# Turning the keys of seven units by VectorE and a trip through DRAM instead of by TensorE

## The chip, the core and the metric

The kernel runs on one core of one Trainium2 chip, in one launch. The metric is the device time of that core in microseconds (us). All data are float32 in the kernel's tiles.

## What is computed

The reference is a gated linear attention, followed by a two-layer MLP with a quick GELU:

```python
# q, k, v, f_logit: (B=4, H=8, S=768, D=48);  moe_w_in (384, 2048);  moe_w_out (2048, 384)
f = 1 / (1 + exp(-f_logit))
for t in range(S):
    state = f[:, :, t, :, None] * state + einsum('bhd,bhe->bhde', k[:, :, t], v[:, :, t])
    y[:, :, t] = einsum('bhd,bhde->bhe', q[:, :, t], state)
x = y.transpose(0, 2, 1, 3).reshape(3072, 384)
h = x @ w_in
out = (h * (1 / (1 + exp(-1.702 * h)))) @ w_out
```

## The kernel before, in words

**Units.** The 3072 tokens are cut into 12 units (NALL) of 256 tokens (U), three for each batch. A unit n goes through `attention(n)`, which gives a list of parts, and later through `mlp_unit(n)`, which gives a list of small matmul jobs, the fill. For n from 4 on, `merge(n, ...)` emits the parts of unit n's attention one by one and, after each part, a share of the fill: the columns of one MLP unit (23040) split in proportion to a number for each kind of part. The fill that runs beside attention n is the end of an older unit's MLP and the beginning of the next. Its jobs come in two sorts. An `h` job (L727) is three matmuls of 256 columns over the three chunks of `w_in`, a sigmoid by ScalarE into `sg` (L732) and a product by VectorE into `g` (L733). An `o` job (L704) is one matmul of 192 columns; seven groups of eight of them, with sums between, make the second layer. In the trace each such float32 matmul leaves two records, so an `h` job shows as 6 and an `o` job as 2.

**Attention of a unit.** Queries, keys and gates of the unit lie in `X` and `F` with feature rows on the partitions and the 4 x 256 columns of 4 pairs of heads (NP) along the free dimension. From unit 3 on (N_FILL), three parts of kind V each do two of the six levels of the scan: scores by TensorE (L384), `promote` by VectorE, which multiplies queries and keys by gates (L439), `evacuate` by VectorE, which masks the scores into `A` (L410), and, one part later, `adds` by TensorE (L448). After the last `promote` the keys in `X[:, 1]` are complete.

**Turning the keys.** The step that brings a unit's keys and values together into states (part S, L523, `pd`) contracts over tokens, so it wants the keys with tokens on the partitions, as the tile `kn`. Two parts of kind T call `turn_k`: four TensorE transpositions of 128x128 into one PSUM tile of the pool tag "mm" (4 buffers, shared with `h` and `o`), then one ScalarE copy of 128x512 into `kn` (L505, L506). `kn` has one buffer, which a later `yT` uses too.

**Starting the next unit.** The parts of kind B of unit n belong to unit n+1. `begin_f` transposes the gates from `raw` into `F` by VectorE (L327, a STREAM_TRANSPOSE of 128x1024 in blocks of 32x32), applies the sigmoid by ScalarE and orders the next unit's gates (4 DMAs on SP's queue); `begin` does so for the queries, with two small GpSimd copies; `begin_k` does it for the keys, into `X[:, 1]`, which is free only when the previous unit's keys have been turned. `begin_k` also copies level 0 aside and makes the first `promote`. `begin_gates`, by GpSimd, multiplies gates together into `tot` (L376).

**The order of a unit n from 4 to 10 before:** V, V, V, B (begin_f, begin of n+1), T, T, B (begin_k of n+1), S (with begin_gates of n+1). The last unit, 11, has V, V, V, T, T, S, W. The shares after each part are those of `steady`.

**Who sets the order.** TensorE executes exactly the order in which the code emits (L89). From L903 on the other engines, SP's DMA queue included, are ordered by a planner, which works with its own costs: an instruction that is ready in its plan can be taken before others that the code emitted earlier but that are not ready. All DMAs that the kernel starts go through one queue, SP's, in the planned order, and an instruction of SP that waits holds those behind it.

**The rest of SP's queue in the stretch around the change:** `vl` (L290) and `vn` (L304), the values of the next unit; `raw` (L258), the next gates, queries and keys; `xT<-yT` (L592, L597), the attention's result on its way to the MLP; `out_dram<-osb` (L765), the result.

Of the kernel before, what the change touches and what calls it, by code (L numbers as in the profile page):

```python
# [9 lines left out]
F32 = mybir.dt.float32  # L10
# [13 lines left out]
def kernel(  # L24
# [33 lines left out]
    nc = tc.nc  # L58
    B, H, S, D = q.shape
    DM = H * D  # L60
    DFF = moe_w_in.shape[1]
    P = 128
    C = 64
    G = 128
    U = 256
    NG = U // G
    NC = U // C
    NU = S // U
    NP = H // 2
# [3 lines left out]
    NK = DM // P  # L73
    NFF = DFF // P
    FG = 4
    PAIRS_AHEAD = 3
    N_FILL = 3
    N_TURN = 2
    NA = NP * U
    NALL = B * NU  # L80
    assert S % U == 0 and NALL % 2 == 0 and NL == 6 and NG == 2 and DM % P == 0 and D <= HS

    const = ctx.enter_context(tc.tile_pool(name="const", bufs=1))
    ld = ctx.enter_context(tc.tile_pool(name="ld", bufs=1))
    att = ctx.enter_context(tc.tile_pool(name="att", bufs=1))
    wp = ctx.enter_context(tc.tile_pool(name="wp", bufs=2))
    mlp = ctx.enter_context(tc.tile_pool(name="mlp", bufs=2))
# [44 lines left out]
    X = const.tile([P, 3, NX], F32, name="X")  # L132
# [6 lines left out]

    w_in = const.tile([P, NK, DFF], F32, name="w_in")  # L140
    w_out = const.tile([P, NFF, DM], F32, name="w_out")
    v_toks = [tc.dram_tile([U, DM], F32, name=f"v_tok{j}") for j in range(2)]
    D2, DR = 2 * D, P - 2 * D
    assert NP == NK + 1 and NK * DR == D2
# [5 lines left out]
    for r in range(NGR):  # L150
        ffs = range(r * FG, (r + 1) * FG)
        for ff in ffs[::2]:
            f = slice(ff * P, (ff + 2) * P)
# [90 lines left out]
    def load_raw(n, j, engine=nc.sync):  # L244
        if n >= NALL:
            return
        b, s0 = n // NU, n % NU * U
        src = (f_logit, q, k)[j]
        if n < N_FILL:
            for a in range(NP):  # L250
                engine.dma_start(
                    out=by_pair[j][32 * a:32 * (a + 1), :, :R * D],
                    in_=src[b, 2 * a:2 * a + 2, s0:s0 + U, :].rearrange("h (i j) d -> i h (j d)", j=R),
                )
            return
        for r in range(4):
            lo = 32 * (r % 2)
            engine.dma_start(  # L258
                out=raw[32 * r:32 * (r + 1), j, :, :R * D - lo],
                in_=src[b, r // 2::2, s0:s0 + U, :].rearrange("a (i j) d -> i a (j d)", j=R)[:, :, lo:],  # L260
            )
# [3 lines left out]
    def order_v(n, engine=nc.sync):  # L265


        if n >= NALL or n < N_TURN:
            return
# [6 lines left out]
    def load_vl(n, l):  # L276

        if n >= NALL:
            return
# [12 lines left out]
    def load_vn(n):  # L292
        if n >= NALL:
            return
# [11 lines left out]
    def rows(h):  # L306
        return slice(h * HS, h * HS + D)
# [5 lines left out]
    def attention(n):  # L313
# [5 lines left out]
        t = {"tms": [F]}  # L319
        parts = []  # L320

        def part(kind):
            return lambda fn: parts.append((kind, fn))
# [174 lines left out]
        def turn_k(a0):  # L498
            if a0 == 0:
                t["kn"] = att.tile([P, NP, NG, P], F32, tag="kn", name=f"kn_{n}", bufs=1)  # L500
            pt = ps.tile([P, 2, NG, P], F32, tag="mm", name=f"tkn_{n}_{a0}", bufs=4)
            for a in range(2):
                for g in range(NG):
                    x = (a0 + a) * U + g * G
                    nc.tensor.transpose(pt[:, a, g, :], X[:, 1, x:x + G], ident)  # L505
            nc.scalar.copy(t["kn"][:, a0:a0 + 2], pt)  # L506

        for a0 in (0, 2):
            part("T")(lambda a0=a0: turn_k(a0))

        @part("S")
        def _():
# [34 lines left out]
        def _():  # L547
# [24 lines left out]
            to_x(lambda h: (yT[rows(h), :NK], lambda r, d: yT[r:r + d, NK]), xT[:, :, :U], NG)  # L572
            if n == NALL - 1:

# [31 lines left out]
    HF, HC = NFF // 2, DM // 2  # L606
    T = {}

    def quarter(w, i, j, ffs=slice(0, HF)):
        return w[:, i * HF + ffs.start:i * HF + ffs.stop, j * HC:(j + 1) * HC]  # L610

    def sums_of_b():


        for i in (1, 2, 3):
            T[i] = wp.tile([P, 2 * DM * 2], I32, tag="bits", name=f"T{i}", bufs=PAIRS_AHEAD)
            T[i] = T[i].bitcast(F32).rearrange("p (f e) -> p f e", f=HF)
        n4 = DM // HC
        t4 = [wp.tile([P, DM], F32, tag="a", name=f"T4_{f}", bufs=4).rearrange("p (f e) -> p f e", f=n4)
              for f in range(0, HF, n4)]  # L620
        T[4] = lambda f: t4[f // n4][:, f % n4]
        sub = lambda *x: nc.vector.tensor_tensor(*x, ALU.subtract)
        h = [slice(f, f + HF // 2) for f in (0, HF // 2)]
        for x in h:
            yield lambda x=x: sub(T[1][:, x], quarter(w_out, 0, 1, x), quarter(w_out, 0, 0, x))
        for x in h:
            yield lambda x=x: sub(T[2][:, x], quarter(w_out, 1, 1, x), T[1][:, x])
        for x in h:
            yield lambda x=x: sub(T[3][:, x], quarter(w_out, 1, 1, x), quarter(w_out, 0, 1, x))
        for i in range(len(t4)):  # L630
            x = slice(i * n4, (i + 1) * n4)
            yield lambda i=i, x=x: sub(t4[i], T[2][:, x], quarter(w_out, 1, 0, x))
# [165 lines left out]
    def mlp_blocks(*blocks):  # L798

        hs, os = zip(*(mlp_block(n, r) for n, r in blocks))  # L800
        return sum(hs, []) + sum(os, [])
# [12 lines left out]
    def parts_of(n):  # L814

        parts = list(units[n][1])
        _, inter = parts.pop()
        if n:
            kind, scores = parts[0]
            _, ahead = units[n - 1][1][-1]  # L820
            parts[0] = kind, lambda: (ahead(), scores())
        if n < N_TURN:

            def with_v(l):
                kind, fn = parts[l]
                return kind, lambda: (fn(), load_vl(n, l) if n == 0 or l else None, keep_up(2 * (n == 0 and l < 3) or 3 * (n == 1 and l == 0)))
            parts[:NL] = [with_v(l) for l in range(NL)]
        if n + 1 < NALL:
            begin_f, begin, begin_k, begin_gates = units[n + 1][0]
            i = len(parts)  # L830
            if n + 1 < N_FILL:

                parts.append(("K", lambda: (begin_k(), begin_gates(), load_vl(n + 1, 0) if n + 1 < N_TURN else None)))
                parts.insert(i - 4, ("B", begin))
                parts.insert(i - 5, ("B", begin_f))
            else:
                kind, states = parts.pop()
                parts += [("B", begin_k), (kind, lambda: (states(), begin_gates()))]
                parts.insert(i - 3, ("B", lambda: (begin_f(), begin())))
        else:  # L840
            parts.append(("W", inter))
        return parts

    def merge(n, fill, columns, share, pieces=0, hold=0, by=1.0, chores=()):

        parts = parts_of(n)
        total = sum(share(kind) for kind, _ in parts)
        converting = {"W": 3, "T": 3, "B": 1} if n < N_FILL - 1 else {"W": 3, "V": 4, "S": 3, "T": 1, "B": 1}  # L850
        total_ops = sum(converting.get(kind, 0) for kind, _ in parts)
        held = sum(share(kind) for kind, _ in parts[:hold])
        at = at_ops = done = ops = 0
        for kind, fn in parts:
            ready = state["done"]
            fn()
            for chore in chores[:2]:
                chore()
            chores = chores[2:]
            at += share(kind)  # L860
            at_ops += converting.get(kind, 0)
            n_ops = min(int(pieces * NOP * at_ops / (by * total_ops)), pieces * NOP) - ops
            ops += n_ops
            first, n_columns = done, max(0, columns * (at - held) / (total - held) - done)

            def some(end):
                nonlocal done
                while fill and done < end and fill[0][2] <= ready:
                    w, emit, _ = fill.pop(0)
                    emit()  # L870
                    done += w
            for i in range(n_ops):
                some(first + n_columns * i / n_ops)
                convert()
            some(first + n_columns)

    def steady(kind):
        return {"W": 3, "V": 4, "S": 3, "T": 1, "B": 1, "K": 1}.get(kind, 0)

    UNIT = NFF * NK * U + U // P * NFF * DM  # L880

    for j in range(3):
# [12 lines left out]
    fill = []  # L895
    merge(0, fill, 0, steady, 8)
    fill += mlp_blocks((0, 0)) + mlp_blocks((0, 1))
    merge(1, fill, UNIT // 2 - LAG // 2, steady, 10, hold=1)
    fill += mlp_blocks((1, 0), (1, 1)) + mlp_blocks((0, 2), (1, 2))
    merge(2, fill, UNIT, steady, 8)  # L900
    fill += mlp_blocks((2, 0), (2, 1)) + mlp_blocks((2, 2), (0, 3)) + mlp_blocks((1, 3), (2, 3))
    merge(3, fill, 3 * UNIT // 2 - LAG // 2, steady, 6, by=0.7)
    fill_order.close()  # L903
    for n in range(3, NALL):
        fill += mlp_unit(n)
    for n in range(4, NALL):
        merge(n, fill, NFF * NK * U + 7 * HF * HC, steady, chores=list(sums_of_b()) if n == 4 else ())
    for _, emit, _ in fill:
        emit()

# [28 lines left out]
```

## Time and profile before

| what | value |
|---|---|
| median of 4 runs | 658.45 us (656.46 to 661.61) |
| the profiled execution | 661.61 us, of which its span is 659.5 us |
| granted TensorE clock | 0.992 |
| TensorE transpositions for `kn` (L505) | x96, mean 273 ns, union of their records 14.1 us |
| ScalarE copies into `kn` (L506) | x24, mean 584 ns |
| VectorE transpositions 128x1024 (L327) | x18 into X, mean 2042 ns; x9 into F, mean 2051 ns |
| ScalarE copies 128x512 from X (L423) | Kc x69, mean 669 ns; Qc x27, mean 641 ns |

The span is the time from the first to the last record on the core. Busy time is the union of an engine's records. A matmul's record is longer than the distance to the next one's start, because matmuls are pipelined; where the cost of some matmuls on a full TensorE is wanted, starts are compared with starts. In the timeline, columns are start, length, engine, line, operation, output and inputs, shapes and count of merged records; in brackets stands the idle time before, with what ended it. The examples are taken from the attention of one late unit, between 335 and 384 us.

### The profile page before, as it was taken

Reading aid. Unit: us, or ns where it says so; the run is one execution under the profiler, and the core shown is the slowest. Engines: PE = TensorE matmul, PEld = TensorE weight load, DVE = VectorE, ACT = ScalarE, POOL = GpSimd, SP = SyncE. Lnnn points to the kernel's source line nnn. Section 1 sums busy time; section 2 is a strip of 40 time slices with the busy share of each in tenths; the row PEclk is TensorE's granted clock in tenths of the full one; section 3 lists DMA queues with packets and bytes.
Section 4 is the critical chain, followed back from the end, with each engine's and each line's share of the span. In section 5 each row is a group of like instructions: output and inputs, shape, how many; then the busy total and the mean of one; then the engine's idle time right before and its main releaser. Section 6 shows DMA issues by size and latency. Waiting matters only on the chain.

```text
span 659.5 us, 20407 instructions
## 1 busy us (share of the span) xinstructions
PE 639.1 (97%) x8964; PEld 545.0 (83%) x8964; DVE 444.8 (67%) x802; ACT 230.1 (35%) x477; POOL 54.0 (8%) x116
## 2 busy tenths in 40 slices
PE   6988999989999999999999999999999999999997
PEld 5655667766677689989989989989989989989997
DVE  2998887688886757657657657658558557553571
ACT  3563543243223423423423424324324324222120
POOL 3020020010001002002002002002002002000000
PEclk9999999999999999999999999999999999999999
DMA  8795973384116453524524434514613202101000
GB/s 184 197 230 155 230 181 96 110 199 98 41 41 176 121 121 95 143 73 99 151 59 116 122 74 119 148 43 119 158 34 95 74 25 59 42 2 25 25 1 24
DMA packets 67554, 67.67 MB, mean 103 GB/s; under 512 B 30410, under 2 KB 61290, under 8 KB 67466
## 3 DMA queue, kind: packets, MB, share of 16 engines
q1 hardware_dynamic: 67466, 66.38, 40.3%
q8 instruction: 70, 1.15, 0.7%
q14 instruction: 18, 0.15, 0.1%
HBM read 56.92 MB, written 8.65 MB: 99 GB/s over the span
## 4 chain that ended last, share of the span: by engine, by line
PE 85%; DVE 7%; DMA 2%; ACT 2%; SPq 2%; issue 1%; DVEq 0%; ACTq 0%
PE h L727 37%; PE o L755 7%; PE o_X L704 7%; PE o_Y L704 7%; PE o_Z L704 7%; PE sc L384 5%; PE y L448 5%; PE o_W L704 4%; PE y L563 2%; PE sc L523 1%; PE tkn L505 1%; DMA xT<-yT 1%; DMA vn<-in_v_dram 1%; DVE X L439 1%; PE t L339 1%
## 5 line engine op out<-in xcount | busy, mean ns | idle before, releaser
L727 PE MATMUL h<-xT,w_in 128*128 128x256 f32 (+1 forms) x1152 | 261.7, 383 | 6.0 <-DMA xT<-yT 3.7
L727 PEld LDWEIGHTS h<-xT,w_in 128*128 128x128 f32 x1152 | 216.4, 191 | 40.3 <-issue 5.0
L733 DVE TENSOR_TENSOR g<-h,sg 128x256 f32<-128x256 f32 (+1 forms) x192 | 80.9, 423 | 101.5 <-ACT sg L732 99.1
L732 ACT ACTIVATE sg<-h 128x256 f32<-128x256 f32 (+1 forms) x192 | 73.2, 383 | 195.8 <-PE h L727 189.0
L423 ACT COPY Kc<-X 128x512 f32<-128x512 f32 x69 | 46.1, 669 | 119.4 <-DVE X L439 83.4
L755 PE MATMUL o<-w_out,g 128*128 128x384 f32 x192 | 66.4, 493 | 0.0
L439 DVE TENSOR_TENSOR X<-X,tot 128x1024 f32<-128x1024 f32 x45 | 55.1, 1225 | 15.4 <-PE sc L384 10.2
L755 PEld LDWEIGHTS o<-w_out,g 128*128 128x128 f32 x192 | 35.2, 190 | 22.8 <-issue 1.5
L704 PE MATMUL o_X<-w_out,g 128*128 128x192 f32 x288 | 51.9, 329 | 0.0
L704 PE MATMUL o_Y<-T,S 128*128 128x192 f32 x288 | 51.1, 331 | 0.1
L704 PEld LDWEIGHTS o_Y<-T,S 128*128 128x128 f32 x288 | 46.5, 190 | 2.5 <-DVE u L679 1.2
L704 PEld LDWEIGHTS o_X<-w_out,g 128*128 128x128 f32 x288 | 47.3, 190 | 0.9
L410 DVE TENSOR_TENSOR A<-sc,masks 128x512 f32<-128x512 f32 x72 | 46.8, 680 | 0.0
L448 PE MATMUL y<-A,vl 64*48 64x64 f32 x2304 | 40.8, 217 | 0.1
L376 POOL TENSOR_TENSOR tot<-F 128x512 f32<-128x512 f32 x12 | 12.5, 1040 | 327.3 <-DVE st L540 327.3
L448 PEld LDWEIGHTS y<-A,vl 64*48 64x48 f32 x2304 | 36.0, 120 | 3.5 <-issue 3.1
L327 DVE STREAM_TRANSPOSE X<-raw 128x1024 f32<-128x1024 f32 x18 | 36.8, 2042 | 2.5 <-PE y L563 2.5
L571 ACT COPY yT<-y 48x512 f32<-48x512 f32 x48 | 27.8, 580 | 13.0 <-PE y L563 12.5
L384 PEld LDWEIGHTS sc<-X,Kc 48*64 48x64 f32 x1344 | 23.9, 134 | 7.1 <-issue 3.4
L384 PE MATMUL sc<-X,Kc 48*64 48x64 f32 x1344 | 28.2, 220 | 0.2 <-DVE A L410 0.2
L376 POOL TENSOR_TENSOR tot<-tot 128x256 f32<-128x256 f32 (+4 forms) x60 | 27.0, 450 | 4.7
L704 PE MATMUL o_Z<-w_out,g 128*128 128x192 f32 x144 | 26.6, 331 | 0.0
(93 smaller groups left out, 664.2 us busy)
## 6 DMA issues: line engine op xcount, KB each, us to landing
vl<-v_tok SPq DMA_DIRECT2D x60, 192.0 KB, 2.8
bits<-in_moe_w_out_dram SPq DMA_DIRECT2D x8, 768.0 KB, 11.1
bits<-in_moe_w_in_dram SPq DMA_DIRECT2D x8, 576.0 KB, 7.0
v_tok<-in_v_dram SPq DMA_DIRECT2D x10, 384.0 KB, 4.3
vn<-v_tok SPq DMA_DIRECT2D x10, 384.0 KB, 6.9
xT<-yT SPq DMA_DIRECT2D x24, 144.0 KB, 2.8
raw<-in_f_logit_dram SPq DMA_DIRECT2D x18, 192.0 KB, 4.2
raw<-in_q_dram SPq DMA_DIRECT2D x18, 192.0 KB, 3.9
```

The costliest lines, as they stand in the source:

```text
L327: nc.vector.transpose(out.rearrange("p (a i j) -> p a j i", a=NP, j=R), raw[:, j].rearrange("p a (j d) -> p (a j) d", j=R)[:, :, :32],)
L376: nc.gpsimd.tensor_tensor(tn, t2[:, :, 0], t2[:, :, 1], ALU.mult)
L384: nc.tensor.matmul(out[g * HS:(g + 1) * HS, h, a, :], lhsT=lhs(h, a * U + g * G), rhs=rhs(h, a * U + g * G), start=True, stop=True,)
L410: nc.vector.tensor_tensor(A[:, :, c:c + w].rearrange("p h (x t) -> p h x t", t=64), t["sc"][:, :, c:c + w].rearrange("p h (x t) -> p h x t ...
L423: nc.scalar.copy(c.rearrange("p (n m) -> p n m", m=m), X[:, j, :NA].rearrange("p (n two m) -> p n two m", two=2, m=m)[:, :, hf, :],)
L439: nc.vector.tensor_tensor(qk, qk, by, ALU.mult)
L448: nc.tensor.matmul(dst(h, g, a), lhsT=vls[n, u][g * 64:(g + 1) * 64, (2 * a + h) * D:(2 * a + h + 1) * D], rhs=A(h, g, a), start=(start an ...
L704: nc.tensor.matmul(t[bank], lhsT=lhs(f), rhs=rhs(f), start=(new and f == 0), stop=(f == HF - 1), skip_group_check=True,)
L727: nc.tensor.matmul(ph, lhsT=w_in[:, c, ff * P:(ff + 1) * P], rhs=xTs[n][:, c, :], start=(c == 0), stop=(c == NK - 1))
L732: nc.scalar.activation(sg, ph, AF.Sigmoid, scale=1.702)
L733: nc.vector.tensor_tensor(g[ff // FG][:, ff % FG, :], ph, sg, ALU.mult)
L755: nc.tensor.matmul(t["po"], lhsT=g[ff // FG][:, ff % FG, tt * P:(tt + 1) * P], rhs=w_out[:, ff, :], start=(ff == ffs[0]), stop=(ff == ffs[ ...
```

## The change

For units 4 to 10 (`CARRY`) the keys are turned in another way. Two VectorE transpositions in 32x32 blocks (one for each group of 128 tokens) write a tile `z`; four DMAs for each carry `z`, 32 partitions at a time, to a DRAM buffer `k_tok` in runs of 512 bytes; one DMA for each group reads it back with tokens on all 128 partitions in runs of 2 KB; one ScalarE copy of 128x512 for each group rearranges it into `kn`. The parts T, T become C (first transposition and its four DMAs) and C2 (second one with its four, and the reading back with the copies). The part B with `begin_f` and `begin` moves behind C2. From unit 4 on, all units use shares of their own, `late`. Units 0 to 3 and 11 keep TensorE's transpositions.

```diff
+    CARRY = range(N_FILL + 1, NALL - 1)
...
+    k_toks = [tc.dram_tile([NG, G, P // 32, 32 * NP], F32, name=f"k_tok{j}") for j in range(2)]
...
-        for a0 in (0, 2):
-            part("T")(lambda a0=a0: turn_k(a0))
+        def carry_k(g):
+            nb = G // 32
+            z = mlp.tile([P, nb, 32, NP], F32, tag="sum", name=f"z_{n}_{g}", bufs=3)
+            nc.vector.transpose(
+                z.rearrange("p b d a -> p a b d"),
+                X[:, 1, :NA].rearrange("p (a g b t) -> p g a b t", a=NP, g=NG, b=nb)[:, g],
+            )
+            for i in range(P // 32):
+                nc.sync.dma_start(
+                    out=k_toks[n % 2][g, :, i].rearrange("(b t) x -> t b x", t=32),
+                    in_=z[i * 32:(i + 1) * 32].rearrange("p b d a -> p b (d a)"),
+                )
+
+        def fetch_k():
+            t["kn"] = att.tile([P, NP, NG, P], F32, tag="kn", name=f"kn_{n}", bufs=1)
+            for g in range(NG):
+                z = mlp.tile([P, P, NP], F32, tag="sum", name=f"kt_{n}_{g}", bufs=3)
+                nc.sync.dma_start(out=z.rearrange("p d a -> p (d a)"), in_=k_toks[n % 2][g].rearrange("t i x -> t (i x)"))
+                nc.scalar.copy(t["kn"][:, :, g, :], z.rearrange("p d a -> p a d"))
+
+        if n not in CARRY:
+            for a0 in (0, 2):
+                part("T")(lambda a0=a0: turn_k(a0))
+        else:
+            parts[-1] = "V3", parts[-1][1]
+            part("C")(lambda: carry_k(0))
+            part("C2")(lambda: (carry_k(1), fetch_k()))
...
-                parts.insert(i - 3, ("B", lambda: (begin_f(), begin())))
+                parts.insert(5 if n in CARRY else 3, ("B", lambda: (begin_f(), begin())))
...
     def steady(kind):
         return {"W": 3, "V": 4, "S": 3, "T": 1, "B": 1, "K": 1}.get(kind, 0)
+
+    def late(kind):
+        return {"V": 7, "V3": 2, "C": 2, "C2": 3, "S": 5, "B": 4, "T": 2, "W": 5}.get(kind, 0)
...
     for n in range(4, NALL):
-        merge(n, fill, NFF * NK * U + 7 * HF * HC, steady, chores=list(sums_of_b()) if n == 4 else ())
+        merge(n, fill, NFF * NK * U + 7 * HF * HC, late, chores=list(sums_of_b()) if n == 4 else ())
```

The new order of a unit from 4 to 10 is V, V, V3, C, C2, B (begin_f, begin), B (begin_k), S.

## The prediction

> **What bounds the kernel now.** I read the page first, for the engine that is full and for the chain that ended last.
>
> ```profile
> PE 639.1 (97%) x8964; PEld 545.0 (83%) x8964; DVE 444.8 (67%) x802; ACT 230.1 (35%) x477; POOL 54.0 (8%) x116
> ...
> PEclk9999999999999999999999999999999999999999
> ...
> PE 85%; DVE 7%; DMA 2%; ACT 2%; SPq 2%; issue 1%; DVEq 0%; ACTq 0%
> ```
>
> TensorE is busy 97% of the span at an even clock, and 85% of the chain is TensorE's. Busy TensorE need not be the limit in every stage, so I next took the windows of one late unit, whose parts repeat every 48.6 to 48.8 us (the first transpositions of units 4 to 10 start at 248.49, 297.30, 345.87, 394.68, 443.44, 492.04 and 540.79).
>
> ```profile
> 335.00:345.00 10.00, 10.00 (x80) 8.79 (x69) 5.38 (x10) 2.52 (x7) 0.00 (x0) 1.00 0.16 41
> 345.00:353.00 8.00, 8.00 (x65) 7.10 (x66) 6.02 (x10) 3.53 (x8) 0.00 (x0) 1.00 0.02 4
> 353.00:360.00 7.00, 7.00 (x154) 6.95 (x146) 5.79 (x10) 1.32 (x3) 2.45 (x5) 1.00 0.84 204
> ```
>
> The columns are window, its length, busy PE, PEld, DVE, ACT, POOL, clock, DMA share and GB/s. TensorE has no gap at all; VectorE is about half idle and the DMA engines nearly empty from 335 to 353, just where the keys are turned. So in these units a microsecond taken off TensorE is a microsecond of the end, as long as nobody makes it wait. The timeline of TensorE there:
>
> ```profile
> 335.40 10.63 PE L727 MATMUL h<-xT,w_in 128*128 128x256 f32 x48
> 345.87 0.60 PE L505 MATMUL tkn<-ident,X 128*128 128x128 f32 x4
> 346.31 2.76 PE L727 MATMUL h<-xT,w_in 128*128 128x256 f32 x12
> 348.90 0.60 PE L505 MATMUL tkn<-ident,X 128*128 128x128 f32 x4
> 349.33 1.46 PE L727 MATMUL h<-xT,w_in 128*128 128x256 f32 x6
> 350.63 2.11 PE L704 MATMUL o_X<-w_out,g 128*128 128x192 f32 x12
> 352.68 1.11 PE L448 MATMUL y<-A,vl 64*48 64x64 f32 x64
> 353.61 1.10 PE L523 MATMUL sc<-vn,kn 64*64 64x48 f32 x64
> ```
>
> **What is removed.** Four transpositions delay the next start by 346.31 - 345.87 = 0.44 us and by 349.33 - 348.90 = 0.43 us. ScalarE's rhythm says the same, with the switches in and out included:
>
> ```profile
> 344.77 0.38 ACT L732 ACTIVATE sg<-h 128x256 f32<-128x256 f32 x1 [0.91 <-PE h L727]
> 346.07 0.38 ACT L732 ACTIVATE sg<-h 128x256 f32<-128x256 f32 x1 [0.91 <-PE h L727]
> 346.50 0.58 ACT L506 COPY kn<-tkn 128x512 f32<-128x512 f32 x1
> 347.80 0.38 ACT L732 ACTIVATE sg<-h 128x256 f32<-128x256 f32 x1 [0.71 <-PE h L727]
> ```
>
> Sigmoids of undisturbed `h` jobs follow each other by 1.30 us, across a group of transpositions by 1.73: 0.435 us for a group. Two groups in each of seven units: 14 x 0.435 = 6.1 us. The Trainium skill would have me take more: "TensorE: Matmul & The Clock Gate", Part 4 on the PE-mode transpose, gives about 275 ns for a 128x128 transposition inside a kernel. The record here is as long (273 ns), but by that price 56 of them would be worth 15.4 us; the trace starts the next work after 109 ns each, so the length is mostly pipeline, and I take 6.1. The 14 PSUM copies of ScalarE (0.58 us each) go too; ScalarE waits for `h` before nearly every sigmoid, so they give nothing.
>
> **What VectorE gets.** Two transpositions of 128x512 per unit. The nearest row is the 128x1024 one at 2042 ns, whose output is also written with a stride: half of it is 1.02 us, and 2.04 if size counted for nothing. I take 1.02; 14.3 us in all. They become ready when the last `promote` of the third V part ends (334.72 + 1.23 = 335.95); afterwards VectorE stands idle 0.87 us before each product of an `h` job, waiting for its sigmoid. So a piece of 1.02 us pushes one product back by about 0.2 us, by 1.2 if it cost 2.04. Does TensorE feel this? An `h` job may take a PSUM buffer again when the product four jobs back is done. That is 3 x 1.30 = 3.9 us after the end of that job, and product and sigmoid need 0.9 of it: 3.0 us are free. The trace tests it: the key transposition of 2.03 us at 349.86 lies among the same products, and TensorE shows no gap there. Cost taken: zero (both bounds stay inside the 3.0). A table of the skill speaks against the change ("VectorE: DVE Perf Modes", Rules for kernel authors): a 128x128 transposition belongs on TensorE where a PSUM destination will do. The rule weighs one operation against another, and by it the old form stands: gain nothing. The windows speak of what is free: TensorE 0.0 of 10 us and VectorE 4.6. I side with the windows.
>
> **What SP and the DMA engines get.** Per unit eight stores of 64 KB and two loads of 256 KB, 1 MB through DRAM. SP issues four loads of `raw` in 1.75 us, so 0.44 us each, 4.4 us for ten. In the timeline SP does nothing between 336.6 and 351.9 us. The price of the chain comes from the median times to landing:
>
> ```profile
> vl<-v_tok SPq DMA_DIRECT2D x60, 192.0 KB, 2.8
> ...
> v_tok<-in_v_dram SPq DMA_DIRECT2D x10, 384.0 KB, 4.3
> vn<-v_tok SPq DMA_DIRECT2D x10, 384.0 KB, 6.9
> ...
> out_dram<-osb SPq DMA_DIRECT2D x18, 192.0 KB, 1.9
> ```
>
> A store of `z` lies nearest to `out_dram<-osb` (SBUF to DRAM, 1.9 us), with `v_tok` (4.3, 384 KB into DRAM in short runs) as the upper end. A load lies nearest to `vl` (the way back from a DRAM buffer); for a third more bytes I take 3.2. Its upper end is `vn`, 6.9, which the timeline issues right behind the four loads of `raw`. Now the clock of one unit, from the end of the third V part's scores and adds at 335.40. By the new shares two `h` jobs follow V3, one C, three C2, four the first B, and one `h` and seven `o` jobs the second. C lies at 335.40 + 2 x 1.30 = 338.0, C2 at 339.3. The first `z` is done at 339.0, the second at 340.8 with a product between; the last of eight stores is issued at 342.1 (340.8 + 3 x 0.44) and lands at 344.0; the second load lands at 347.2. The copy into `kn` reads SBUF like the `Kc` copies, 0.67 us (0.58 if it were like the old ones): 347.9. `pd` wants `kn` at 353.61 - 0.87 (transpositions gone) + 0.34 (one `o` job more ahead of S than before) = 353.1. Cover 5.2 us. So the new wait of `pd` costs nothing. With the upper load, 6.9, 1.5 remain; with both upper ends (2.4 more) it is 0.9 us late.
>
> **What waits behind the waits.** SP's loads wait for the stores to land (344.0). Behind them stand the four `raw` loads of keys, two `vl` and one `vn`: now at 351.9 to 355.2, and wanted a unit later. If the planner puts the `raw` loads in between, the second load of keys runs behind them; that is the 6.9 above. ScalarE's copy waits for the load, and behind it stand the sigmoids; the 3.0 us of PSUM cover hold there. Traffic of 1 MB lies where the DMA share is 0.02 to 0.16.
>
> **What is moved.** `begin_f` and `begin` go behind C2, with two VectorE transpositions, one sigmoid, two GpSimd copies and eight `raw` loads, past the ten new DMAs. In the trace these two run ahead of their place in the code: the gates' transposition at 358.31 is released by GpSimd's `tot`, the queries' at 361.88 by `y`, both some 20 to 25 us before the third V part (scores at 382.23) behind which the code puts them. Their place sets nothing, cost zero; if that cover were gone, the two of 2.05 us would stand together among products, 1.1 us over the 3.0. `begin_k` no longer waits for TensorE and can start 7 us earlier, off the bounding chain: worth nothing. The shares put 25 instead of 26 `o` jobs behind the first V part and 7 instead of 6 ahead of S; the sum of the fill is the same, and 0.2 to 0.3 us less beside the first V part is small beside the 3 us between the last copy there (368.6) and the next scores (371.6).
>
> **The sum.** -6.1 + 0. The profiled execution's 661.61 (span 659.5, 2.1 around it) becomes 655.5. That execution lies 3.2 above the median of the four; the saving is TensorE work at the same clock, so from the median: 658.45 - 6.1 = 652.4.
>
> **The rivals.**
> *The keys come late to `pd`.* For it: the load can stand behind 736 KB of `raw`, some rows there take up to 8.0 us (176 KB of keys), and TensorE, in fixed order, loses every microsecond. Against: SP and DMA engines are empty for 15 us. With a store of 4.3 and a load of 8.0 `kn` comes at 342.1 + 4.3 + 8.0 + 0.67 = 355.1, 2.0 late: 7 x (2.0 - 0.87) = +7.9, so 666.4. It decides from 0.87 us on (nothing gained) and makes the kernel measurably slower from 1.34.
> *ScalarE is held by the copy.* If the plan sets the copy early because it thinks the DMAs quick, ScalarE stands, sigmoids wait, and past 3.0 us `h` stops. A hold of 3.6 us eats 0.6 of 0.87 per unit: 658.45 - 7 x 0.27 = 656.6. For it: two landings in a row; against: 3.0 us free.
> *The work removed was not on the end.* If the unit's pace were VectorE's, nothing would come: 658.5. Against: VectorE's 33 of 49 us in a unit, now 35.
>
> **How the numbers follow.** Differences within 0.5% (3.3 us) are about what a measurement of this kernel cannot tell from none. Full gain, with 2 us of scatter each way: 0.60, 650.4 to 654.4. More than that, from better packing: 0.03. Held ScalarE or keys late by up to 1.34 us: 0.13; work not on the end: 0.04; together 655.2 to 661.7. Keys late by more: 0.20, 662 to 672. Faster 0.63, same 0.17, slower 0.20. From 649.5 to 664 I leave out 0.02 below and about 0.16 above.
>
> **What would show it.** Right: TensorE without gaps around S, unit period near 47.8 us, `kn` copies ending some 5 us before `pd`, 14 VectorE transpositions near 1.02 us. Wrong: `pd` released by the copy or its DMA, idle TensorE at `h` released by `g`, ScalarE idle with a DMA as releaser, landings of `k_tok` above 4 us. The prediction fails if those waits pass 0.87 us a unit.

## The result, and the profile after

The changed kernel takes 655.61 us (median; 653.71 to 659.24) against 657.86 us of the kernel before: a ratio of 0.997, 95% interval 0.9959 to 0.9981, so about 2.0 us less (1.3 to 2.7). The forecast was 6.1 less. A third of it came, and the experiments show that even this third is not the forecast one.

One thing must be set right first. By the text of the change above, the new order holds for units 4 to 10 and the new shares from unit 4 on. The diff's line `parts.insert(i - 3, ...)`, now `parts.insert(5 if n in CARRY else 3, ...)`, acts on more: `i` is the number of parts at that point. It is 6 in unit 3, so nothing changes there, but 9 in unit 2, whose six levels are six parts. There the part that begins unit 3's gates and queries moved from place 6 to place 3. The prediction overlooked this.

The page of the profile after, the lines for busy time and for the chain that ended last:

```profile
PE 630.2 (97%) x8908; PEld 537.2 (82%) x8908; DVE 458.2 (70%) x816; ACT 232.5 (36%) x477; POOL 55.2 (8%) x116
...
PE 80%; DVE 13%; issue 3%; ACT 2%; DMA 1%; SPq 1%; DVEq 0%; ACTq 0%
```

TensorE has less to do, as wanted, but in the chain TensorE's share fell from 85% to 80% and VectorE's rose from 7% to 13%. The windows of one late unit (columns as before):

```profile
330.00:340.00 10.00, 9.40 (x44) 7.95 (x43) 8.99 (x14) 3.92 (x10) 0.00 (x0) 1.00 0.65 181
340.00:350.00 10.00, 10.00 (x171) 9.22 (x170) 5.69 (x12) 3.58 (x7) 0.00 (x0) 1.00 0.25 62
```

A gap of 0.60 us in TensorE that was not there, in a window in which VectorE is 90% busy and which is followed by one with VectorE 57% busy. It returns once in each of the seven units. The waits of the whole run for `g` (us in total, times, longest; PEld are TensorE's weight loads):

```profile
PEld h L756 <- DVE g L762: 7.7, 8, 1.0
...
PE h L756 <- DVE g L762: 4.5, 8, 0.6
```

Seven of the eight are these; the eighth, early in the run, is in the kernel before too. So `h` waits for a PSUM buffer that the product `g` has to give back. TensorE's timeline of that unit:

```profile
328.90 5.45 PE L756 MATMUL h<-xT,w_in 128*128 128x256 f32 x24
334.94 9.33 PE L756 MATMUL h<-xT,w_in 128*128 128x256 f32 x42 [0.60 <-DVE g L762]
344.11 2.44 PE L733 MATMUL o_X<-w_out,g 128*128 128x192 f32 x14
346.48 1.11 PE L450 MATMUL y<-A,vl 64*48 64x64 f32 x64
347.41 1.10 PE L552 MATMUL sc<-vn,kn 64*64 64x48 f32 x64
```

The 24 records are four `h` jobs, which take all four PSUM buffers. One job takes 1.295 us (the sigmoids of undisturbed jobs follow each other at that distance, 337.00 to 346.07 for seven of them in the kernel before). Without a wait the fifth job would start at 328.90 + 4 x 1.295 = 334.08; it starts at 334.94, 0.86 us late. (The bracket shows less, because the records of the four run on to 334.35, beyond the next possible start.) So 0.86 us was lost against 0.87 saved. VectorE in the same stretch:

```profile
329.35 1.28 DVE L412 TENSOR_TENSOR A<-sc,masks 128x512 f32<-128x512 f32 x2
330.55 2.02 DVE L515 STREAM_TRANSPOSE z<-X 128x512 f32<-128x512 f32 x2
332.60 2.03 DVE L329 STREAM_TRANSPOSE X<-raw 128x1024 f32<-128x1024 f32 x1
334.48 0.73 DVE L762 TENSOR_TENSOR g<-h,sg 128x256 f32<-128x256 f32 x2
```

The masking of the scores, both transpositions of the carried keys, and the next unit's key transposition stand in one block of 5.1 us. In the kernel before, the same masking is followed by a product, and the next unit's key transposition comes 14 us later, after TensorE's transpositions, among the last products:

```profile
335.86 1.28 DVE L410 TENSOR_TENSOR A<-sc,masks 128x512 f32<-128x512 f32 x2
337.42 0.42 DVE L733 TENSOR_TENSOR g<-h,sg 128x256 f32<-128x256 f32 x1 [0.28 <-ACT sg L732]
...
349.86 2.03 DVE L327 STREAM_TRANSPOSE X<-raw 128x1024 f32<-128x1024 f32 x1
```

After the change, the product of the first of those four `h` jobs is ready at 330.92 (its sigmoid runs from 330.50 to 330.88) and starts at 334.48, 3.56 us late. The fifth job starts 0.04 us after that product ends (334.48 + 0.42 = 334.90), so for a start at 334.08 the product had to end by 334.04: it could have been 2.70 us late at no cost. This is the cover meant below. 3.56 - 2.70 = 0.86.

The late keys that the prediction feared did not come. SP's queue and ScalarE's copies of the same unit:

```profile
331.67 3.73 SPq L520 DMA_DIRECT2D k_tok<-z  x8
335.56 0.34 SPq L529 DMA_DIRECT2D kt<-k_tok  x1
335.94 0.44 SPq L260 DMA_DIRECT2D raw<-in_k_dram  x1
336.78 0.34 SPq L529 DMA_DIRECT2D kt<-k_tok  x1
337.16 1.41 SPq L260 DMA_DIRECT2D raw<-in_k_dram  x3
```

```profile
339.77 1.14 ACT L530 COPY kn<-kt 128x512 f32<-128x512 f32 x1 [0.26 <-DMA kt<-k_tok]
...
342.00 1.11 ACT L530 COPY kn<-kt 128x512 f32<-128x512 f32 x1
```

The second copy ends at 343.11, 4.3 us before `pd` wants it at 347.41, though a copy takes 1.12 us and not 0.67 as the prediction took.

Because the first 200 us scatter from run to run by some us in the profiles, the late part is best read from the starts of `pd` (first line of the scores from `vn` and `kn`) in each profiled execution. Working: unit 4's start from unit 10's, and unit 10's from the end of the span.

| kernel | from unit 4 to 10, us | per unit | from unit 10 to the end |
|---|---|---|---|
| before | 548.53 - 256.22 = 292.31 | 48.72 | 110.97 |
| after | 542.19 - 250.14 = 292.05 | 48.68 | 110.51 |

The late units gained 0.04 us each, not 0.87.

### The profile page after: what moved, and what is told of

The parts are those of the page before. It is cut to its first block, busy times and chain, and to the rows that moved or that the text cites. A ratio compares the mean times of both kernels' runs of the same rounds, so it can differ in the third digit from the quotient of the medians.

```text
span 652.7 us, 20424 instructions
## 1 busy us (share of the span) xinstructions
PE 630.2 (97%) x8908; PEld 537.2 (82%) x8908; DVE 458.2 (70%) x816; ACT 232.5 (36%) x477; POOL 55.2 (8%) x116
## 4 chain that ended last, share of the span: by engine, by line
PE 80%; DVE 13%; issue 3%; ACT 2%; DMA 1%; SPq 1%; DVEq 0%; ACTq 0%
PE h L756 32%; PE o_Y L733 8%; PE o_X L733 7%; PE o L784 7%; PE o_Z L733 7%; PE sc L386 5%; PE o_W L733 4%; PE y L450 4%; DVE X L329 2%; PE t L341 2%; DVE z L515 2%; DVE A L412 2%; PE y L592 2%; PE sc L552 1%; DVE s L221 1%
## 5 line engine op out<-in xcount | busy, mean ns | idle before, releaser
L762 DVE TENSOR_TENSOR g<-h,sg 128x256 f32<-128x256 f32 (+1 forms) x192 | 79.5, 421 | 74.8 <-ACT sg L761 73.2
```

Source lines behind the costliest of these rows:

```text
L762: nc.vector.tensor_tensor(g[ff // FG][:, ff % FG, :], ph, sg, ALU.mult)
```

## Experiments

Twelve kernels ran. Ratios are to the kernel before on the same chip, whose median was 659.17 us in the first group (e1 to e4), 658.29 in the second (e5 to e8) and 659.41 in the third (e9 to e12). Intervals are 95%.

**e1_hold_k: the next unit's key transposition back among the products.** `issue_after` keeps what it encloses behind the named instruction in its engine's order; it adds no wait. Below, this is called a hold.

```diff
-            turn(2, X[:, 1, :NA])
+            if n - 1 in CARRY:
+                with tc.issue_after(last["g"].ins):
+                    turn(2, X[:, 1, :NA])
...
-                nc.vector.tensor_tensor(g[ff // FG][:, ff % FG, :], ph, sg, ALU.mult)
+                last["g"] = nc.vector.tensor_tensor(g[ff // FG][:, ff % FG, :], ph, sg, ALU.mult)
```

> The changed kernel, but the next unit's key transposition (2.03 us) is queued behind the last product that the code emitted before it; the two transpositions of the carried keys stay where they are. Block theory (three transpositions, 4.05 us, stand behind the masking of the scores on VectorE, the first product comes 3.6 us late, PSUM covers 3.0, so TensorE loses 0.56 us in each of seven units): the block shrinks to 2.05 us, the gap at h goes, 655.6 - 3.9 = 651.7. Rival, the transpositions of TensorE were worth only 2.2 us: no gap to close, 655.6. Rival, DMA traffic or the longer ScalarE copies (1.12 us each) hold the unit: 655.6.

Measured: 651.07 us, ratio 0.9881 (0.9857 to 0.9906). Its late units take 47.84 us each, 0.88 less than before: the whole forecast gain. VectorE's timeline of the unit:

```profile
332.55 1.28 DVE L416 TENSOR_TENSOR A<-sc,masks 128x512 f32<-128x512 f32 x2
333.75 2.02 DVE L519 STREAM_TRANSPOSE z<-X 128x512 f32<-128x512 f32 x2
335.62 0.73 DVE L766 TENSOR_TENSOR g<-h,sg 128x256 f32<-128x256 f32 x2
...
346.11 2.03 DVE L329 STREAM_TRANSPOSE X<-raw 128x1024 f32<-128x1024 f32 x1
```

and TensorE's 11 `h` jobs in a row, without a wait (66 records, 332.10 to the next start at 346.45):

```profile
332.10 14.51 PE L760 MATMUL h<-xT,w_in 128*128 128x256 f32 x66
```

The edit changes nothing but the place of seven instructions of VectorE, and the gap is gone. The rivals that leave the time at 655.6 (the removal being worth little, DMA traffic, the longer ScalarE copies) fall. What hangs on the held transposition moves with it, though: the load of `raw` that stood between the two loads of keys now comes behind both. The next run keeps it between.

**e2_hold_z: the other way to break the block.** The transposition in `carry_k` is put under `with tc.issue_after(last["g"].ins)`, the next unit's keys are left to the planner.

> The changed kernel, but each of the two transpositions of the carried keys is queued behind the last product emitted before it, as the order of the code has them; the next unit's key transposition is left to the planner. Block theory: no two of the three stand together any more, no product is more than 2.1 us late, no gap at h: 651.7. Rivals (worth of the removal, DMA, ScalarE copies): 655.6.

Measured: 650.46 us, ratio 0.9861 (0.9838 to 0.9885), 47.84 us per unit. VectorE:

```profile
335.57 1.10 DVE L516 STREAM_TRANSPOSE z<-X 128x512 f32<-128x512 f32 x1
336.53 0.41 DVE L763 TENSOR_TENSOR g<-h,sg 128x256 f32<-128x256 f32 x1
336.86 1.10 DVE L516 STREAM_TRANSPOSE z<-X 128x512 f32<-128x512 f32 x1
...
338.73 2.01 DVE L329 STREAM_TRANSPOSE X<-raw 128x1024 f32<-128x1024 f32 x1
```

Here the next unit's key transposition is early, as in the changed kernel, with a load of `raw` between the two loads of keys (issued at 340.98), and does no harm: products stand between, and the 11 `h` jobs take 14.51 us as in e1. It is the block, not the early place.

**e3_shares: the shares alone.** `CARRY = range(0)` in the changed kernel.

> The changed kernel with no unit carried (TensorE turns all keys, as before), so only the new shares of the fill remain. Block theory: 657.9, no difference. Rival, the new shares cost what is missing: 657.9 + 3.9 = 661.8.

Measured: 660.65 us, ratio 1.0023 (1.0008 to 1.0038): 1.5 us slower, so neither of the two numbers that were expected. Its late units take 49.22 us, 0.50 more than before, with a wait of another kind (us, times, longest):

```profile
PE o_Y L733 <- DVE u L708: 2.7, 6, 0.5
```

This kernel has V, V, V, B, T, T, B, S under `late`, a mixture that the changed kernel doesn't contain, and it also has unit 2's change, so it can't be subtracted from the others. The wait is not in the changed kernel's list with that count, so the shares don't explain the missing gain there.

**e4_removed: the removal alone.** In the kernel before, `turn_k` of units 4 to 10 leaves out the transpositions and lets ScalarE copy the keys unturned, so the states of these units come from wrong numbers. Nothing is carried, and the shares are the old ones:

```diff
+            if N_FILL < n < NALL - 1:
+                nc.scalar.copy(t["kn"][:, a0:a0 + 2], X[:, 1, a0 * U:(a0 + 2) * U].rearrange("p (a g t) -> p a g t", a=2, g=NG))
+                return
```

> The kernel before, with the TensorE transpositions of units 4 to 10 left out: ScalarE copies the keys unturned into the tile instead (so the states of these units are computed from wrong numbers), nothing is carried, the shares are the old ones. It measures the removal alone. Block theory and the sum of the prediction: 14 groups of 0.435 us, 657.9 - 6.1 = 651.8. Rival, the removal is worth only 2.2 us: 655.6.

Measured: 652.47 us, ratio 0.99 (0.9878 to 0.9921), or 6.6 us less (5.2 to 8.0); 47.84 us per unit, 0.88 below before. The term of 6.1 us was right. Here too the next unit's keys are freed early: their transposition stands at 334.90 behind the masking alone, the first product comes about 1.5 us late, and TensorE loses nothing.

**e5_unit2: the line that I had overlooked, alone.** In the kernel before:

```diff
-                parts.insert(i - 3, ("B", lambda: (begin_f(), begin())))
+                parts.insert(3, ("B", lambda: (begin_f(), begin())))
```

> The kernel before with one line of the change alone: the part that starts the next unit's gates and queries goes to place 3 of every unit's list. That differs from before only in unit 2, which has nine parts, and where the order of all engines is the written one. Theory: this is the part of the gain of the four kernels so far that the late units do not show (in their traces the state products of unit 4 came 2 to 6 us earlier than in before, but that scatters); sum 6.1 + 1.5 - 6.0 = 1.6 to 2.2 for the change. Expected 1.5 below the kernel before. Rival: scatter of the early stretch, 0.

Measured: 655.86 us, ratio 0.9962 (0.9947 to 0.9977), 2.5 us less (1.5 to 3.5), with late units as before (48.71). It is a loss of the same kind: VectorE pieces in a row hold up what TensorE waits for, here by way of ScalarE. The kernel before, VectorE, ScalarE and TensorE, ahead of unit 2's state products:

```profile
130.76 2.04 DVE L327 STREAM_TRANSPOSE F<-raw 128x1024 f32<-128x1024 f32 x1
132.63 2.03 DVE L327 STREAM_TRANSPOSE X<-raw 128x1024 f32<-128x1024 f32 x1
```

```profile
132.89 1.06 ACT L332 ACTIVATE F<-F 128x1024 f32<-128x1024 f32 x1 [2.51 <-DVE F L327]
...
134.12 0.58 ACT L506 COPY kn<-tkn 128x512 f32<-128x512 f32 x1
```

```profile
132.83 0.60 PE L505 MATMUL tkn<-ident,X 128*128 128x128 f32 x4
134.75 2.86 PE L727 MATMUL h<-xT,w_in 128*128 128x256 f32 x12 [1.32 <-ACT kn L506]
```

Gates and queries are transposed one behind the other; ScalarE waits for the gates, with its copy of `kn` queued behind, and TensorE waits for the PSUM buffer that this copy gives back. With the one line changed:

```profile
129.13 0.60 PE L505 MATMUL tkn<-ident,X 128*128 128x128 f32 x4
129.56 2.76 PE L727 MATMUL h<-xT,w_in 128*128 128x256 f32 x12
```

That gap of 1.32 us is in the profiles of before, e4, e9 and e11, which have the old line, and in none of the ten others. It accounts for 1.3 of the 2.5 us; where the rest comes from is not shown.

**e6_after: the changed kernel again**, beside the second group.

> The changed kernel unaltered, beside the others on the same chip. Expected ratio 0.997 to the kernel before, and 1.007 to 1.010 to the kernel with the next unit's key transposition held.

Measured: 654.97 us, ratio 0.9951 (0.9934 to 0.9969), 48.67 us per late unit. By the intervals, nothing beyond e5's gain is left for the carrying.

**e7_long3: a dose.** e1 with longer transpositions of the carried keys, the first done twice: `z` gets `nb + 2` blocks of which the stores read `nb`, and the transposition stands in `for _ in range(2 - g)`.

> The kernel with the next unit's key transposition held, and VectorE's two transpositions of the carried keys made half as long again (they also turn blocks that nobody reads), the first of them done twice. Planned order: masking, two of 1.6 us, one product, one of 1.6 us, next product. Block theory, with a first product that may start 2.7 us late: masking 1.28 + 3.2 makes it 2.9 late, the second one after it 3.6 late, against 2.7 each: 0.9 us lost in each of seven units, 6.3 above the kernel with the hold alone. Rival, VectorE's work as such costs nothing wherever it stands or costs by its sum (2.7 us more in a unit with 14 us idle): no difference from that kernel.

Measured: 657.5 us, ratio 0.9988 (0.9967 to 1.0009). That is the expected time, but for the most part not for the expected reason. VectorE, ScalarE and TensorE in the unit's stretch of `h`:

```profile
333.29 2.97 DVE L521 STREAM_TRANSPOSE z<-X 128x768 f32<-128x768 f32 x2
336.07 0.44 DVE L768 TENSOR_TENSOR g<-h,sg 128x256 f32<-128x256 f32 x1
336.41 1.57 DVE L521 STREAM_TRANSPOSE z<-X 128x768 f32<-128x768 f32 x1
337.82 0.74 DVE L768 TENSOR_TENSOR g<-h,sg 128x256 f32<-128x256 f32 x2
```

```profile
333.23 0.38 ACT L767 ACTIVATE sg<-h 128x256 f32<-128x256 f32 x1 [3.10 <-PE h L762]
334.53 0.38 ACT L767 ACTIVATE sg<-h 128x256 f32<-128x256 f32 x1 [0.91 <-PE h L762]
```

```profile
338.29 1.81 PEld L762 LDWEIGHTS h<-xT,w_in 128*128 128x128 f32 x9 [0.32 <-DVE g L768]
...
331.63 14.70 PE L762 MATMUL h<-xT,w_in 128*128 128x256 f32 x66
```

11 `h` jobs take 14.70 us, against 14.51 in e1: 0.19 lost and not 0.9. The first product (ready at 333.65, 0.04 us after its sigmoid, as above) starts at 336.07, 2.42 us late and inside the cover; the second (ready at 334.95) starts at 337.82, 2.87 late and 0.17 beyond it. The other six units say the same: the second product is 2.77 to 2.87 late, and 0.09 to 0.19 is lost. So the dose came out smaller than planned, but where it passes the cover TensorE loses the excess. Most of the time went elsewhere in the unit:

```profile
313.95 4.19 PE L739 MATMUL o_Y<-T,S 128*128 128x192 f32 x16 [1.87 <-DVE u L714]
```

The planner has put the sum `u` (L714) behind two promotions and a masking, and the second `o_Y` group waits for it. So the whole time of this run can't stand for the block; it also shows that a change of one duration can make the planner order another place worse.

**e8_last and e12_last: both holds (of e1 and e2), and unit 11 carried too.** `CARRY` to `NALL`, and for unit 11 a share of 12 behind C2.

> The changed kernel with both holds (carried keys and next unit's keys each behind the last product emitted before them), and unit 11 carried too, with a share of 12 behind its C2 so that its keys have some 10 us to come back. Theory: as the kernels with one hold, and 0.87 less for the eighth unit: 0.987 of the kernel before. Rival: the last unit's keys come late, as there is little else to run beside it: 0.5 to 2 us above the kernel with the hold.

> Both holds and unit 11 carried too, once more, beside the kernel with both holds on one chip. Theory: 0.8 us less than that kernel, which is at the edge of what the rounds can tell. Rival: no gain, the last unit's work beside it is too short.

Measured: 650.22 us, ratio 0.9881 (0.985 to 0.9912), and 651.44 us, ratio 0.9885 (0.9853 to 0.9916). In the profiles unit 10 to the end takes 109.75 and 109.71 us against 110.55 in e10 below: 0.8 less, as expected, but the medians don't resolve it.

**e9_late_only: both holds without unit 2's change.** As e10, with `5 if n in CARRY else i - 3`.

> Both holds, and unit 2's list as it was before (the part with its gates and queries at its old place). What is left is the carrying in units 4 to 10 and the shares. Theory: 6.1 from the transpositions taken off TensorE and some 0.5 at the last units, 0.990 of the kernel before. Rival, the holds help by something else than the seven gaps: 0.987 or less even without unit 2.

Measured: 653.4 us, ratio 0.9916 (0.9884 to 0.9948), 5.5 us less (3.4 to 7.6); 47.94 us per late unit. This is the change that was forecast, without the block and without the bonus.

**e10_both: both holds.**

> The changed kernel with both holds: carried keys and next unit's keys each behind the last product emitted before them. Theory: no gap is left for the second hold to close, so as with one hold, 0.987 of the kernel before, and 2.4 (unit 2) below the kernel without unit 2's change.

Measured: 652.37 us, ratio 0.9887 (0.9861 to 0.9913), 47.89 us per late unit. The second hold adds nothing to one.

**e11_z_only: VectorE's extra work alone.** In the kernel before, `turn_k` of units 4 to 10 also transposes into an unused `z`.

> The kernel before with the two VectorE transpositions of each unit from 4 to 10 added, their result unused: TensorE still turns the keys, so the next unit's keys still wait for it and stand 11 us later. Theory: the block is masking 1.28 + 2.1, the first product 1.6 late against 2.7, so no difference: 1.000 of the kernel before. Rival, VectorE's extra 2.1 us in a unit cost as such: up to 14 us above.

Measured: 658.69 us, ratio 0.9992 (0.9976 to 1.0008), 48.71 us per late unit. The 14 transpositions cost nothing as such. Masking and both of them stand in one block here too, but the next unit's keys, still tied to TensorE, do not:

```profile
333.61 1.28 DVE L410 TENSOR_TENSOR A<-sc,masks 128x512 f32<-128x512 f32 x2
334.81 2.05 DVE L503 STREAM_TRANSPOSE z<-X 128x512 f32<-128x512 f32 x2
336.69 0.76 DVE L739 TENSOR_TENSOR g<-h,sg 128x256 f32<-128x256 f32 x2
```

The first product is 1.5 us late, well inside the cover.

The best versions are the change with a hold. e1, e2, e8, e10 and e12 can't be told from each other by their intervals; each beats both kernels: their intervals end at 0.9916 at most, the changed kernel's begin at 0.9934.

## Why the prediction was wrong

*What is removed: right.* e4 measured 6.6 us (5.2 to 8.0) for the forecast 6.1, and 0.88 per unit. The price from distances of starts held. The other price that the prediction weighed, 275 ns each (the Trainium skill, "TensorE: Matmul & The Clock Gate", Part 4, which gives it for bf16), would have made 15.4 us and did not hold as a price in a stream.

*What VectorE gets: the step that failed.* The prediction put the cost of VectorE's new work to TensorE at zero. It priced each piece by itself ("a piece of 1.02 us pushes one product back by about 0.2 us"), placed the two pieces by the order of the code, "with a product between", and said of the next unit's keys that `begin_k` "can start 7 us earlier, off the bounding chain: worth nothing". Both transpositions (1.10 us each) were released by the last promotion, as I said, and the next unit's keys by the second of them, because no TensorE transposition had to be waited for any more. So they came ready one right after the other, and the planner put them in one row behind the masking, which the prediction did not count: 1.28 + 2.02 + 2.03 with their overlaps, 5.1 us. The sum that should have been made is that row against the cover. The prediction made just this sum for the gates and queries (two of 2.05, 1.1 over the 3.0), but not for the keys. The transposition that it took as a test, one of 2.03 us among products, says nothing of a row of four. The cover was 2.70 us and not 3.0, because the 0.3 us from the end of a job's 1.295 us on TensorE (328.90 + 1.295 = 330.20) to its sigmoid (330.50) was left out, a small error; the missing term was 7 x 0.86 = 6.0. The wait itself, TensorE idle at `h` and released by `g`, stood among the prediction's signs of being wrong. e1 and e2 take it away by order alone; e11 shows that the row without its last member is free, e4 the same without the two pieces, and e7 that beyond the cover the excess is lost. And the table's rule that the prediction set aside, by which nothing is to be gained, did not hold for this kernel: e9 gained 5.5 us (3.4 to 7.6).

*SP and the DMA engines: right in kind.* No wait of `pd` for the keys, 4.3 us of cover against 5.2 forecast. Eight stores were issued in 3.73 us, 0.47 each. The planner did put a load of `raw` between the two loads of keys, and the copies took 1.12 us, 0.45 more than taken; the cover bore both. None of the three rivals came true in the late units, though VectorE's part of the last one, that it would set the unit's pace, was near: it did so for 0.86 us at one place. That 655.6 falls into the range given to late keys and a held ScalarE (655.2 to 661.7) is chance; neither happened.

*What is moved: wrong in one place.* I read the place of the part as 3 for every unit; in unit 2 it was 6. That line is worth 2.5 us (1.5 to 3.5) by e5.

*The shares:* from unit 10 to the end 0.46 us was gained (110.97 to 110.51), not forecast. The profiles with the old shares (before, e4, e5, e11) show 110.92 to 110.98 there, those with the new ones and unit 11 not carried 110.51 to 110.55, or 109.97 in e3.

The sum now: -6.1 + 6.0 - 2.5 - 0.5 = -3.1. Measured were -2.0 (1.3 to 2.7) and, in e6, -3.2 (2.0 to 4.3). The difference to the first is within what e5's interval leaves open, so the sum is consistent with both and not finer than about 1 us. Why the planner counted the block as harmless can't be seen in a trace, only the order it gave.

## What to carry to other kernels

Work moved to an engine with idle time is free only where it stands: add up everything that becomes ready at the same event on that engine, with what already stands there, and set the sum against the buffers of the engine that must not wait. When a change removes a dependency, look at what that dependency was holding back; here it had kept 2 us of VectorE work out of a block at no cost. And read an index of a list for every list that passes through it, not for the ones the change is about.

## What the runs showed of the hardware

A VectorE transposition of float32 in 32x32 blocks, with a strided output, has a record of 1.10 us for 128x512, 1.57 for 128x768 (e7) and 2.03 for 128x1024. In a row the next instruction starts before the record's end: 0.92 (2.02 - 1.10), 1.40 (2.97 - 1.57) and 1.88 us (334.48 - 332.60) after the start. By these three sizes that is 1.8 ns for each element of a partition, and hardly any fixed cost. A ScalarE copy of 128x512 that reads its source with a stride of four elements took 1.12 us, against 0.67 for the copies aside of `Kc`, 0.62 for e4's copies into the same tile and 0.58 from PSUM. Eight stores of 64 KB and the first load of 256 KB back from DRAM took 8.1 us from the first issue (331.67) to the start of the first copy (339.77).
